# Second product of batch 1 by Strassen's algorithm as well, with a new order of the slots around it, the read-out transpose three steps later, and the last tile's column halves in two banks

## The chip, the cores and the metric

The kernel runs on one core of one Trainium2 chip. The metric is the device time in microseconds (us) of one execution; lower is better. A profile of one execution is shown beside it. Engines are named as the profile names them: PE (matmuls), PEld (its weight loads), DVE (vector), ACT (activations), POOL (GpSimd), SP (which issues DMAs). DMAs issued by POOL convert f32 to bf16 on the way.

## The reference

Attention of 8 batches between 512 tokens and 32 state rows (8 heads of 64), in both directions, and a feed-forward layer on the result:

```python
scores  = softmax(x @ state^T / 8);  xread = scores @ state     # 512 rows a batch
scores2 = softmax(state @ x^T / 8);  sread = scores2 @ x        #  32 rows a batch
rows = concat(xread, sread)          # (8*544, 512) over all heads
h = rows @ w_in                      # w_in  512 x 2048
out = gelu(h) @ w_out                # w_out 2048 x 512, exact gelu
```

## The kernel before

**One batch's path.** `rearr` (POOL, two copies) puts a loaded batch `xb` into the layout that `xtr_dma` (a DMA transpose issued by SP) turns into `xT`; `rearr_ones` puts it into a second layout `xo` for the read-out. `scores` multiplies `xT` by the state and lets ACT take exp into `e`; `norm(b, half)` (DVE: sum `cs`, reciprocal `ics`, product) makes the normalised weights `a`; `atr_dma` (SP, DMA transpose) or `atr` (PE) turns them into `AT`. Instead of forming `xread`, the kernel folds the state into `w_in` first: `p_mm` and `p_copy` make P of a batch in four chunks of 512 columns, `pmat(b, f)` or several in one `burst`; ACT copies one half of a chunk, DVE the other. The first product of hidden block m is then P^T times `AT`, two matmuls into a bank `hp` and a gelu by ACT into `g`. `M(16b+m, ...)` is that, mostly in pairs.

**The second product, plainly.** `U(u)` is a quarter (4 of 16 hidden blocks) of one of the four 128-row output tiles, four matmuls of 512 columns; after a tile's fourth quarter DVE copies the bank to `osb` and SP sends it out. Batch 0 does some of it block by block (`mm2_m`). Batches 0 and 1 are done in this way.

**The second product by Strassen.** Batches 2 to 7 split `g` and `w_out` into two by two blocks and make seven products, `X(b, name)`, 16 matmuls of 256 columns each. Their operands are sums of blocks: `g_sum` for g (DVE, one per batch and name), `w_sums` for the weights (five, once). ACT and DVE copy the products `s3`, `s34`, `q`, `oh`; POOL makes `u` and `v`; DVE adds the last ones to the bank's content. The weight sums lie in the storage of batch 0's input buffers (tags `mix0` to `mix3`).

**The read-out rows.** `sread` (PE), `sread_out` (DVE: `inv`, `srm`), then `srt`: a PE transpose into an `f` bank and a DVE copy into `XSR`. All 256 of these rows go through both products late in batch 7 (`mm1_sr`, `R`).

**Order.** Nothing is scheduled by a tool: each engine runs its instructions in the order in which the program emits them, waiting on semaphores. A batch's slot has eight steps p with one pair M each; with the pair of step p run pieces of the previous batch's second product and the next batch's preparation. In the loop over batches 2 to 7, products 4, 5, 1, 2, 7 of the batch before go with steps 0 to 4, and products 3 and 6 of the batch itself with steps 6 and 7. The slot of batch 2 before the change has two, later one, pieces U of batch 1 with steps 0 to 4, and batch 1's own slot is written out by hand with U 12 to U 22 of batches 0 and 1.

**Banks and buffers.** [...] four in turn for `hp`, `pt`, `sr`, `srT`, `p_ps` and other short uses (pool `ps_f`), four named o0 to o3 for output tiles, Strassen products and some P chunks. `xb`, `AT`, `P`, `g` have two buffers each.

**Loads.** POOL issues the loads in its own order with its copies. `hold` is a copy of one column of `g` on POOL: it makes the loads behind it wait for a certain gelu.

**The end.** For batch 7, L4, L5, L2, L1 and L7 take the place of the X products; L1 and L7 share the banks of each 128-row tile j (L7 adds on), L7 makes tile 1 in two column halves, and each half is added to `u` and sent out.

Of the kernel before, what the change touches and what calls it, by code (L numbers as in the profile page):

```python
# [17 lines left out]
def kernel(  # L18
# [84 lines left out]
    def load_w_in(f0, f1):  # L103
        for t in range(2):
            nc.gpsimd.dma_start(  # L105
                out=w_in_bf[64 * t:64 * t + 64, :, f0:f1],
                in_=moe_w_in[256 * t:256 * t + 256, f0:f1].rearrange("(c d) f -> d c f", c=HC),
            )
# [3 lines left out]
    def load_w_out(i):  # L112
        nc.gpsimd.dma_start(out=w_out_bf[:, 4 * i:4 * i + 4, :], in_=w_out_r[:, 4 * i:4 * i + 4, :])

    def load_x(b):
        xb = xin.tile([128, H, SJ * D], BF16, name="xb", tag="xb")
        nc.gpsimd.dma_start(out=xb, in_=xr[b])
        xbs[b] = xb
# [13 lines left out]

    def load_rest():
        load_w_out(1)
        for f in range(2, FC):
            load_w_in(512 * f, 512 * f + 512)
            load_w_out(f)
        load_st(2, B)
        load_x(2)
        load_x(3)  # L140


    def keep_warm(n):
# [288 lines left out]

    def burst(chunks, b_read=None):
        done = []
        first = len(chunks) < 4 and b_read is not None
        if first:
            sread(b_read)
        for i, (b, f) in enumerate(chunks):  # L440
            done.append((b, f, p_mm(b, f, ftile if i < 2 else otile)))
        for x in done[:2]:
            p_copy(*x)
        if b_read is not None and not first:
            sread(b_read)
        for x in done[2:3]:
            p_copy(*x)
        if b_read is not None:
            sread_out(b_read)
        for x in done[3:]:  # L450
            p_copy(*x)


    def pmat00(h):
        if h == 0:
            Ps[0] = att.tile([128, 2, d_ff], BF16, name="P", tag="P")
# [42 lines left out]
    def mm2(b, q, j):  # L499
        if q == 0:  # L500
            ops[b, j] = otile([128, d_model], "op")
        ps = ops[b, j]
        for m in range(4 * q, 4 * q + 4):
            nc.tensor.matmul(  # L504
                ps,
                lhsT=gs[b][:, m, j * 128:(j + 1) * 128],
                rhs=w_out_bf[:, m, :],
                start=(m == 0),
                stop=(m == MC - 1),
            )  # L510
        if q == 3:
            rows = out_rows(b, j)
            evac(ps, [(rows, slice(0, 128), 0, d_model)])

    def mm1_sr(m):
        hp = ps_f.tile([128, B * NS], FP32, name="hps", tag="f")
# [162 lines left out]
    def L2():  # L679
# [5 lines left out]
        xs[b, "v"] = c_tile("v")  # L685
        nc.vector.tensor_tensor(out=xs[b, "v"], in0=xs[b, "y"], in1=c21, op=ALU.subtract)

    def L1():
        b = B - 1
        for j in range(2):  # L690
            ps = xs[b, "x", j] = otile([128, 1, NH], "xp", 2 - 2 * j)
            x_mm(ps, xs[b, "g1"], w_sum["1"], True, (j,))
            nc.vector.tensor_tensor(
                out=xs[b, "o", 1][:, j, right],
                in0=ps[:, 0, :],
                in1=xs[b, "v"][:, j, :],
                op=ALU.add,
            )
        rows_out(1, both, right, nc.sync)

    def L7():
        b = B - 1
        o = xs[b, "o", 0]
        h = NH // 2
        for j, pieces in ((0, ((0, NH),)), (1, ((0, h), (h, NH)))):
            ps = xs[b, "x", j]
            for n0, n1 in pieces:
                for m in range(MH):
                    nc.tensor.matmul(
                        ps[:, 0, n0:n1],  # L710
                        lhsT=xs[b, "g7"][:, m, 128 * j:128 * j + 128],
                        rhs=w_sum["7"][:, m, n0:n1],
                        start=False,
                        stop=(m == MH - 1),
                        skip_group_check=True,
                    )
                nc.vector.tensor_tensor(
                    out=o[:, j, n0:n1],
                    in0=ps[:, 0, n0:n1],
                    in1=xs[b, "u"][:, j, n0:n1],  # L720
                    op=ALU.add,
                )
                eng = nc.scalar if j and n0 else nc.sync
                rows_out(0, slice(j, j + 1), slice(n0, n1), eng)

    rs = {}

# [67 lines left out]
            nc.vector.tensor_tensor(out=rs["o", 0][:, :NH], in0=ps, in1=rs["u"], op=add)  # L795
            r_out(0)

    def p_run(b, fs, banks):
        done = []
        for f, at in zip(fs, banks):  # L800
            it = iter(at or ())
            tiles = (lambda shape, name: otile(shape, name, next(it))) if at else ftile
            done.append((b, f, p_mm(b, f, tiles)))
        for x in done:
            p_copy(*x)


    def M(*ms):
# [77 lines left out]
    srt(0)  # L886
    U(4, 5)
    rearr_ones(1)
    U(6)
    pmat(0, 2)  # L890
    norm(1, 0)
# [4 lines left out]
    sread_out(1)  # L896
    M(10, 11)
    mm2_m(0, 8)
    mm2_m(0, 9)
    burst([(0, 3), (1, 0)])  # L900
    mm2_m(0, 10)
    atr(1)
    M(12, 13)
    srt(1)
    M(14, 15)
    mm2_m(0, 11)
    begin(2)
    rearr(2)
    xtr_dma(2)
    rearr_ones(2)  # L910
    U(12)
    burst([(1, 1), (1, 2)])
    U(13)
    state_prep(2, B)
    M(16, 17)
    U(14)
    M(18, 19)
    U(15)
    burst([(1, 3), (2, 0), (2, 1)])
    U(16)  # L920


    u = 17
    for p in range(2, 8):
        if p == 4:
            scores(2, 0)
            scores(2, 1)
            norm(2, 0)
            norm(2, 1)
        if p == 7:  # L930
            atr_dma(2)
        if p == 3:
            begin(3)
            rearr(3)
            xtr_dma(3)
            rearr_ones(3)
        M(16 + 2 * p, 17 + 2 * p)
        U(u)
        u += 1
        if p in (5, 7):  # L940
            pmat(2, 2 + p // 7)
        if p >= 3:
            w_sums(p - 3)
        if p == 2:
            nc.gpsimd.tensor_copy(out=hold, in_=gs[1][:, 4, 0:1])
            load_x(4)

    for b in range(2, B):
        nb = b + 1
        for p in range(8):  # L950
            k = 16 * b + 2 * p
            if p == 1 and nb < B:
                scores(nb, 0)
                scores(nb, 1)
            if p in (2, 3) and nb < B:
                norm(nb, p - 2)
            if p == 3 and nb + 1 < B:
                xtr_dma(nb + 1)
            if p == 5 and nb < B:
                atr_dma(nb)  # L960
            if p == 3 and nb < B:
                srt(b)
            if p == 7 and nb == B - 1:
                srt(nb)
            M(k, k + 1)
            if b == 2:
                for _ in range(2 if p < 4 else 1):
                    if u < 32:
                        U(u)
                        u += 1  # L970
            elif p < 5:
                if p == 0:
                    g_sum(b - 1, "5")
                X(b - 1, "45127"[p])
                if p < 3:
                    g_sum(b - 1, "127"[p])
            if nb == B and p < 4:
                for m in range(4 * p, 4 * p + 4):
                    mm1_sr(m)
            if p == 1 and nb < B:  # L980
                sread(b)
                sread_out(b)
            if p == 4 and nb == B - 1:
                sread(nb)
                sread_out(nb)
            if p == 0 and b + 3 < B:
                nc.gpsimd.tensor_copy(out=hold, in_=gs[b][:, 0, 0:1])  # L987
                load_x(b + 3)
            if p == 0 and nb + 1 < B:
                begin(nb + 1)  # L990
                rearr(nb + 1)
            if p == 2 and nb + 1 < B:
                rearr_ones(nb + 1)
            if nb == B:
                if p == 4:
                    r_homes()
                    r_sum("5")
                    r_sum("2")
                if p == 5:
                    g_sum(b, "6")  # L1000
                    R("3")
                    r_sum("1")
                    R("4")
                    r_sum("6")
                    r_sum("7")
                if p == 6:
                    R("5")
                    X(b, "3")
                    R("2")
                    R("1")  # L1010
                if p == 7:
                    R("6")
                    X(b, "6")
                continue
            if p == 5:
                g_sum(b, "6")
                if nb < B:
                    p_run(nb, (0, 1), ((0, 1), (3, 2)))
            if p == 6:
                X(b, "3")  # L1020
            if p == 7:
                if nb < B:
                    p_run(nb, (2, 3), ((1, 2), None))
                X(b, "6")
# [41 lines left out]
```

The softmax here doesn't subtract the row's maximum and nothing guards it: scores larger than these inputs give would overflow.

## Time and profile before

| | us |
|---|---|
| median of 7 runs (209.31 to 210.76) | 210.44 |
| the profiled execution: its own time | 209.73 |
| its span, first to last instruction | 208.0 |

| engine | busy, us | share |
|---|---|---|
| PE | 200.3 | 96% |
| DVE | 137.3 | 66% |
| ACT | 133.1 | 64% |
| PEld | 131.1 | 63% |
| POOL | 61.8 | 30% |

Starts and durations below come from the profiled execution. A PE row names a run of matmuls: its length ends with the last matmul's modelled end, so the step from one row's start to the next row's start is what a block takes of PE. In brackets stand the idle time ahead of a row and what ended it. A row `SPq` is the time in which SP issues a DMA, not the time until the data have landed; that is told by the view of a tile or of the DMA issues.

### The profile page before, as it was taken

What the parts mean: (1) busy time and instruction counts of PE and PEld (TensorE: products, weight loads), DVE (VectorE), ACT (ScalarE), POOL (GpSimd) and SP (SyncE); (2) the same over time, 40 slices, a digit from 0 to 9 for tenths busy, and PEclk for the clock granted to TensorE, in tenths of its full rate; (3) what the DMA queues carried; (4) which work ended last, traced back from release to release, by engine and by line L of the source; (5) the groups of instructions that cost most, each with busy time, mean ns of one, the idle gap of its engine ahead of it and who ended that gap; (6) DMA issues with size and microseconds to landing.
All of it is one profiled execution on the core that took longest, in us unless ns stands there. A gap on an engine that the chain in (4) does not pass through costs nothing.

```text
span 208.0 us, 4691 instructions
## 1 busy us (share of the span) xinstructions
PE 200.3 (96%) x1963; PEld 131.1 (63%) x1971; DVE 137.3 (66%) x218; ACT 133.1 (64%) x240; POOL 61.8 (30%) x69
## 2 busy tenths in 40 slices
PE   7799999998999999999999999999999999999993
PEld 7545444443454567756775677657775788778882
DVE  2944675747919649995699658855887553165872
ACT  3864865679794779565956777587757566744120
POOL 8964301663171015710577005500220001200000
PEclk9999999999999999999999999999999999999999
DMA  6999999789283908736681603360106001030124
GB/s 193 192 178 204 206 196 194 139 201 186 50 101 97 259 0 102 155 128 77 72 179 40 169 0 82 74 202 3 52 3 202 3 0 50 3 151 0 54 102 151
DMA packets 40261, 23.14 MB, mean 111 GB/s; under 512 B 21808, under 2 KB 38320, under 8 KB 40240
## 3 DMA queue, kind: packets, MB, share of 16 engines
q0 software_dynamic: 13936, 8.10, 28.5%
q1 hardware_dynamic: 25616, 14.36, 26.4%
q10 hardware_dynamic: 688, 0.39, 0.6%
q8 instruction: 15, 0.25, 0.5%
q14 instruction: 6, 0.05, 0.1%
HBM read 17.30 MB, written 8.91 MB: 126 GB/s over the span
## 4 chain that ended last, share of the span: by engine, by line
PE 79%; DVE 12%; POOL 4%; ACT 3%; issue 1%; POOLq 0%; DVEq 0%; ACTq 0%
PE xp L586 28%; PE hp L478 22%; PE op L504 9%; DVE gsum L580 5%; PE p_ps L415 5%; PE op L531 3%; PE hps L518 3%; PE rp L764 3%; DVE a L347 2%; POOL w_in_bf L105 2%; DVE cs L344 1%; PE sr L378 1%; PE pt L324 1%; POOL sbd L95 1%; ACT g L485 1%
## 5 line engine op out<-in xcount | busy, mean ns | idle before, releaser
L485 ACT ACTIVATE g<-hp 128x512 bf16<-128x512 f32 x124 | 67.6, 603 | 31.6 <-PE hp L478 26.5
L478 PE MATMUL hp<-AT,P 128*128 128x512 bf16 x248 | 64.2, 379 | 0.5 <-DVE XSR L405 0.4
L586 PEld LDWEIGHTS <-gsum 128*128 128x128 bf16 x464 | 45.0, 98 | 11.5 <-issue 2.1
L580 DVE TENSOR_TENSOR gsum<-g 128x2048 bf16<-128x2048 bf16 x30 | 39.3, 1327 | 0.1
L478 PEld LDWEIGHTS <-P 128*128 128x128 bf16 x248 | 22.2, 98 | 21.2 <-issue 4.0
L586 PE MATMUL xp<-ws,gsum 128*128 128x256 bf16 x272 | 32.5, 273 | 0.0
L427 DVE CAST P<-p_ps 128x512 bf16<-128x512 f32 x31 | 20.0, 683 | 16.0 <-PE p_ps L415 16.0
L504 PE MATMUL op<-w_out_bf,g 128*128 128x512 bf16 x90 | 23.0, 379 | 0.3
L586 PE MATMUL xp<-ws,g 128*128 128x256 bf16 x192 | 22.9, 273 | 0.0
L586 PE MATMUL xp<-w_out_bf,gsum 128*128 128x256 bf16 x192 | 22.8, 273 | 0.0
L586 PEld LDWEIGHTS <-g 128*128 128x128 bf16 x192 | 18.8, 98 | 4.3
L426 ACT CAST P<-p_ps 128x512 bf16<-128x512 f32 x31 | 17.0, 604 | 6.8 <-PE p_ps L415 6.8
L635 POOL TENSOR_TENSOR u<-s,oh 128x512 f32<-128x512 f32 x5 | 6.3, 1265 | 49.0 <-ACT oh L632 49.0
L504 PEld LDWEIGHTS <-g 128*128 128x128 bf16 x96 | 9.1, 98 | 11.5 <-issue 1.1
L218 POOL COPY x<-xb 128x1024 bf16<-128x1024 bf16 x12 | 12.6, 1082 | 11.1 <-DMA xb<-in_x_dram 11.1
L228 POOL COPY xo<-xb 128x1024 bf16<-128x1024 bf16 x12 | 14.5, 1242 | 1.3 <-PE sr L378 1.3
L347 DVE TENSOR_TENSOR a<-e,ics 128x512 bf16<-128x512 bf16 x14 | 13.9, 995 | 0.5
L415 PE MATMUL p_ps<-w_in_bf,sbd 64*32 64x512 bf16 x248 | 11.5, 382 | 0.8 <-ACT g L485 0.7
L344 DVE TENSOR_REDUCE cs<-e 128x16 f32<-128x512 bf16 x14 | 9.5, 676 | 3.8 <-ACT e L331 3.8
L605 POOL TENSOR_TENSOR v<-q,oh 128x512 f32<-128x512 f32 x5 | 6.4, 1275 | 14.8 <-ACT oh L637 14.8
L629 DVE TENSOR_TENSOR s<-xp,s 128x512 f32<-128x512 f32 x5 | 3.5, 692 | 11.0 <-PE xp L586 11.0
L987 POOL COPY hold<-g 128x1 bf16<-128x1 bf16 x3 | 1.0, 331 | 31.5 <-ACT g L485 31.5
(111 smaller groups left out, 220.5 us busy)
## 6 DMA issues: line engine op xcount, KB each, us to landing
xb<-in_x_dram POOLq DMA_DIRECT2D x7, 512.0 KB, 6.7
out_dram<-oh SPq DMA_DIRECT2D x13, 256.0 KB, 2.4
out_dram<-osb SPq DMA_DIRECT2D x10, 256.0 KB, 3.2
out_dram<-oh SPq DMA_DIRECT2D x5, 512.0 KB, 2.8
w_out_bf<-in_moe_w_out_dram POOLq DMA_DIRECT2D x4, 512.0 KB, 12.7
w_in_bf<-in_moe_w_in_dram POOLq DMA_DIRECT2D x6, 256.0 KB, 12.0
x0f<-in_x_dram SPq DMA_DIRECT2D x3, 256.0 KB, 4.0
w_in_bf<-in_moe_w_in_dram POOLq DMA_DIRECT2D x4, 128.0 KB, 4.2
```

The source lines that it names most:

```text
L218: nc.gpsimd.tensor_copy(out=A.x4[:, :, :, 64 * t:64 * t + 64].rearrange("p j c d -> p c j d"), in_=src[:, t],)
L228: eng.tensor_copy(out=A.xo[:, :, :, 2 + 64 * t:66 + 64 * t].rearrange("p j c d -> p c j d"), in_=src[:, t],)
L344: nc.vector.reduce_sum(out=cs, in_=e4, axis=AX.X)
L347: nc.vector.tensor_tensor(out=A.a[:, :, hs].rearrange("p g (c n) -> p g c n", n=NS), in0=e4, in1=ics[:, :, :].to_broadcast((128, G, 2, NS) ...
L415: nc.tensor.matmul(ps[t][32 * c:32 * c + 32, :], lhsT=sbd[64 * t:64 * t + 64, b, c, 32 * t:32 * t + 32], rhs=w_in_bf[64 * t:64 * t + 64, c ...
L426: nc.scalar.copy(out=dst[:, 0, :], in_=ps[0])
L427: nc.vector.tensor_copy(out=dst[:, 1, :], in_=ps[1])
L478: nc.tensor.matmul(hp, lhsT=Ps[b][:, t, m * 128:(m + 1) * 128], rhs=atts[b].AT[:, :, t, :], start=(t == 0), stop=(t == 1),)
L485: nc.scalar.activation(out=gs[b][:, m, :], in_=hp, func=AF.Gelu)
L504: nc.tensor.matmul(ps, lhsT=gs[b][:, m, j * 128:(j + 1) * 128], rhs=w_out_bf[:, m, :], start=(m == 0), stop=(m == MC - 1),)
L580: nc.vector.tensor_tensor(out=t, in0=g_q(b, h0, k0), in1=g_q(b, h1, k1), op=op)
L586: nc.tensor.matmul(ps[:, j - js[0], :], lhsT=lhs[:, m, 128 * j:128 * j + 128], rhs=rhs[:, m, :], start=(first and j == js[0] and m == 0), ...
```

## The change

- Batch 1's second product is made by the X products: 3 and 6 in its own slot, 4, 5, 1, 2, 7 in steps 0 to 4 of batch 2's slot, as for the batches after it. Its sixteen pieces U and their four evictions go.
- The slots of batches 0 (its end) and 1 are written in another order: the first pair of batch 1 comes before blocks 12 to 15 of batch 0; P's chunks, which came in bursts of two or three, come singly but for the first two of batch 1, and the last two chunks of batch 2 move into batch 2's slot; chunk 3 of batch 1 is copied by DVE alone (`p_copy_v`).
- Weight sums start earlier: sum 6 during batch 0, sums 3, 4 and 1 in batch 1, sum 7 in batch 2.
- Loads: x(2) goes ahead of the last quarter of `w_out`, the state of batch 2 is loaded alone ahead of it; x(3) and the rest of the state come after a hold on a gelu of batch 1, x(4) at step 0 of batch 2 in place of batch 1's third step, x(5) at step 6 of batch 2 in place of step 0. The rest is as it was.
- The evacuation of batch 0's last output tile goes out in two column halves.
- `srt(b)` moves from step 3 to step 6.
- In the tail, L1 and L7 take three pieces (tile 0 whole, tile 1 in two column halves) with a bank for each.

```diff
     def load_rest():
         load_w_out(1)
-        for f in range(2, FC):
-            load_w_in(512 * f, 512 * f + 512)
-            load_w_out(f)
-        load_st(2, B)
+        load_w_in(1024, 1536)
+        load_w_out(2)
+        load_w_in(1536, 2048)
+        load_st(2, 3)
         load_x(2)
-        load_x(3)
+        load_w_out(3)
...
-            evac(ps, [(rows, slice(0, 128), 0, d_model)])
+            h = d_model // 2 if j == SJ - 1 else d_model
+            evac(ps, [(rows[:, n:n + h], slice(0, 128), n, n + h) for n in range(0, d_model, h)])
...
+    PIECES = ((0, 0, NH, 2), (1, 0, NH // 2, 0), (1, NH // 2, NH, 1))
...
     def L1():
-        for j in range(2):
-            ps = xs[b, "x", j] = otile([128, 1, NH], "xp", 2 - 2 * j)
-            x_mm(ps, xs[b, "g1"], w_sum["1"], True, (j,))
+        for j, n0, n1, at in PIECES:
+            ps = xs[b, "x", j, n0] = otile([128, n1 - n0], "xp", at)
+            l_mm(ps, "1", j, n0, n1, True)
...
+    def p_copy_v(b, f, ps):
+        for t in range(2):
+            nc.vector.tensor_copy(out=Ps[b][:, t, f * 512:(f + 1) * 512], in_=ps[t])
+
+    def hold_for(b, m):
+        nc.gpsimd.tensor_copy(out=hold, in_=gs[b][:, m, 0:1])
...
     rearr_ones(1)
+    w_sums(2)
     U(6)
...
     mm2_m(0, 8)
+    p_run(1, (0, 1), (None, None))
     mm2_m(0, 9)
-    burst([(0, 3), (1, 0)])
+    atr(1)
+    pmat(0, 3)
     mm2_m(0, 10)
-    atr(1)
+    M(16, 17)
+    srt(1)
     M(12, 13)
-    srt(1)
-    M(14, 15)
     mm2_m(0, 11)
     begin(2)
     rearr(2)
     xtr_dma(2)
+    M(14, 15)
+    state_prep(2, 3)
+    pmat(1, 2)
+    hold_for(0, 15)
     rearr_ones(2)
     U(12)
-    burst([(1, 1), (1, 2)])
+    w_sums(0)
+    M(18, 19)
+    hold_for(1, 3)
+    load_x(3)
+    load_st(3, B)
     U(13)
-    state_prep(2, B)
-    M(16, 17)
+    w_sums(1)
+    M(20, 21)
+    scores(2, 0)
+    scores(2, 1)
+    w_sums(3)
     U(14)
-    M(18, 19)
+    p_run(1, (3,), ((3, 0),), p_copy_v)
+    begin(3)
+    rearr(3)
+    xtr_dma(3)
+    rearr_ones(3)
+    M(22, 23)
+    norm(2, 0)
+    M(24, 25)
+    p_run(2, (0,), ((1, 3),))
     U(15)
-    burst([(1, 3), (2, 0), (2, 1)])
-    U(16)
-    u = 17
-    for p in range(2, 8):
...
+    norm(2, 1)
+    X(1, "3")
+    atr_dma(2)
+    g_sum(1, "6")
+    M(26, 27)
+    M(28, 29)
+    p_run(2, (1,), ((1, 2),))
+    state_prep(3, B)
+    M(30, 31)
+    X(1, "6")
...
-            if p == 3 and nb < B:
+            if p == 6 and nb < B:
                 srt(b)
...
             M(k, k + 1)
-            if b == 2:
-                for _ in range(2 if p < 4 else 1):
-                    if u < 32:
-                        U(u)
-                        u += 1
-            elif p < 5:
+            if b == 2 and p in (0, 3):
+                pmat(2, 2 + p // 3)
+            if b == 2 and p == 1:
+                w_sums(4)
+            if p < 5:
...
             if p == 0 and b + 3 < B:
-                nc.gpsimd.tensor_copy(out=hold, in_=gs[b][:, 0, 0:1])
-                load_x(b + 3)
+                hold_for(b, 0)
+                load_x(4 if b == 2 else b + 3)
+            if p == 6 and b == 2:
+                hold_for(b, 12)
+                load_x(5)
```

More of the change, by code (lines that the diff above doesn't have):

```diff
@@ L430, in pmat @@
         p_copy(b, f, p_mm(b, f, ftile))
[L435 to L451, printed above, removed]
     def pmat00(h):
@@ L686, in L2, with l_mm @@
         nc.vector.tensor_tensor(out=xs[b, "v"], in0=xs[b, "y"], in1=c21, op=ALU.subtract)
+    PIECES = ((0, 0, NH, 2), (1, 0, NH // 2, 0), (1, NH // 2, NH, 1))
+    def l_mm(ps, name, j, n0, n1, first):
+        for m in range(MH):
+            nc.tensor.matmul(
+                ps,
+                lhsT=xs[B - 1, "g" + name][:, m, 128 * j:128 * j + 128],
+                rhs=w_sum[name][:, m, n0:n1],
+                start=(first and m == 0),
+                stop=(m == MH - 1),
+                skip_group_check=True,
+            )
     def L1():
         b = B - 1
-        for j in range(2):
-            ps = xs[b, "x", j] = otile([128, 1, NH], "xp", 2 - 2 * j)
-            x_mm(ps, xs[b, "g1"], w_sum["1"], True, (j,))
+        for j, n0, n1, at in PIECES:
+            ps = xs[b, "x", j, n0] = otile([128, n1 - n0], "xp", at)
+            l_mm(ps, "1", j, n0, n1, True)
             nc.vector.tensor_tensor(
-                out=xs[b, "o", 1][:, j, right],
-                in0=ps[:, 0, :],
-                in1=xs[b, "v"][:, j, :],
+                out=xs[b, "o", 1][:, j, NH + n0:NH + n1],
+                in0=ps,
+                in1=xs[b, "v"][:, j, n0:n1],
                 op=ALU.add,
@@ L702, in L7 @@
         b = B - 1
[L703 to L724, printed above, removed]
+        for j, n0, n1, at in PIECES:
+            ps = xs[b, "x", j, n0]
+            l_mm(ps, "7", j, n0, n1, False)
+            nc.vector.tensor_tensor(
+                out=xs[b, "o", 0][:, j, n0:n1], in0=ps, in1=xs[b, "u"][:, j, n0:n1], op=ALU.add
+            )
+            rows_out(0, slice(j, j + 1), slice(n0, n1), nc.scalar if n0 else nc.sync)
     rs = {}
@@ L796, in R, with p_run @@
             r_out(0)
-    def p_run(b, fs, banks):
+    def p_run(b, fs, banks, copy=None):
         done = []
@@ L804, in p_run @@
         for x in done:
-            p_copy(*x)
+            (copy or p_copy)(*x)
+    def p_copy_v(b, f, ps):
[3 more added lines that the diff above has]
+        nc.gpsimd.tensor_copy(out=hold, in_=gs[b][:, m, 0:1])
     def M(*ms):
@@ L909 @@
     xtr_dma(2)
+    M(14, 15)
+    state_prep(2, 3)
+    pmat(1, 2)
+    hold_for(0, 15)
     rearr_ones(2)
     U(12)
-    burst([(1, 1), (1, 2)])
-    U(13)
-    state_prep(2, B)
-    M(16, 17)
-    U(14)
-    M(18, 19)
-    U(15)
-    burst([(1, 3), (2, 0), (2, 1)])
-    U(16)
-    u = 17
-    for p in range(2, 8):
[L925 to L937, printed above, removed]
-        U(u)
-        u += 1
[L940 to L946, printed above, removed]
+    w_sums(0)
[3 more added lines that the diff above has]
+    load_st(3, B)
+    U(13)
+    w_sums(1)
[3 more added lines that the diff above has]
+    w_sums(3)
+    U(14)
+    p_run(1, (3,), ((3, 0),), p_copy_v)
[7 more added lines that the diff above has]
+    p_run(2, (0,), ((1, 3),))
+    U(15)
+    norm(2, 1)
[8 more added lines that the diff above has]
+    X(1, "6")
     for b in range(2, B):
@@ L965 @@
             M(k, k + 1)
-            if b == 2:
-                for _ in range(2 if p < 4 else 1):
-                    if u < 32:
-                        U(u)
-                        u += 1
-            elif p < 5:
+            if b == 2 and p in (0, 3):
[3 more added lines that the diff above has]
+            if p < 5:
                 if p == 0:
```

## The prediction

> **What bounds the kernel now.** I read the page's busy times, then its slices, then its chain, then the waits and the timelines by engine.
>
> ```profile
> PE 200.3 (96%) x1963; PEld 131.1 (63%) x1971; DVE 137.3 (66%) x218; ACT 133.1 (64%) x240; POOL 61.8 (30%) x69
> ...
> PE   7799999998999999999999999999999999999993
> ...
> PE 79%; DVE 12%; POOL 4%; ACT 3%; issue 1%; POOLq 0%; DVEq 0%; ACTq 0%
> ```
>
> PE is busy 96%; its one slice under 9 after the start is the tenth, near 50 us. So the bound is PE's own work plus few waits, and an edit is worth the matmul time it takes away plus the waits it takes away or makes. The timelines of PE (two rows), DVE and SP:
>
> ```profile
> 50.19 0.90 PE L415 MATMUL p_ps<-w_in_bf,sbd 64*32 64x512 bf16 x8 [0.67 <-ACT g L485]
> ...
> 90.40 0.59 PE L478 MATMUL hp<-AT,P 128*128 128x512 bf16 x2 [0.17 <-DVE XSR L405]
> ```
> ```profile
> 89.63 0.72 DVE L405 COPY XSR<-srT 128x128 bf16<-128x128 bf16 x1
> 89.97 0.90 DVE L608 TENSOR_TENSOR oh<-xp,v 128x512 f32<-128x512 f32 x1
> 90.78 0.68 DVE L643 TENSOR_TENSOR oh<-xp,u 128x512 f32<-128x512 f32 x1
> ```
> ```profile
> 46.89 3.18 SPq L271 DMA_TRANSPOSE xT<-x  x1
> 51.14 1.55 SPq L367 DMA_TRANSPOSE AT<-a  x1
> ```
>
> The first shows PE held while ACT switches tables for batch 2's exp. The second shows the first product waiting for the PSUM tile of srT, which DVE drains only after its normalising work; then the two adds of the Strassen product free the banks that P's matmuls want. The third shows that the transpose AT of batch 2 is issued by SP only behind xT of batch 3. It lands 3.1 to 3.4 us after issue (the view by tile), so near 54.4; the batch's first matmul starts at 55.11. **AT is nearly late already.**
>
> [...] xT holds SP 1.9 to 3.2 us and lands 4.4 to 6.4 us after issue. [...] one DVE multiply for `a` takes 0.69 us at 49 us and 1.57 at 84 us beside POOL's copies. [...] the clock is full throughout.
>
> **Prices, from starts on the PE timeline.** A pair of hidden blocks (4 matmuls, `M`) or a second-product piece (`U`) 0.864 us. A Strassen product (16 of 256 columns, `X`) 1.75. A chunk of P (8 matmuls) 0.44, and 0.22 for each further one in the same burst.
>
> **The change, part by part.**
> (1) Batch 1's second product: 16 U, 13.82 us, become 7 X, 12.25: PE -1.57. P's chunks lose bursts: before 0.66+0.66+0.87+0.44+0.44 = 3.07, after 0.66 and seven single, 3.74: +0.67. Net -0.90 of PE work. DVE gains 5 sums of 1.15 to 1.8 and four adds of 0.7 for four evictions dropped; ACT gains 3 copies of 0.59 and hands one P copy to DVE; POOL gains two adds of 1.27. DVE is 66% and ACT 64% busy; where that cover fails is in (3).
>
> (2) From 27.52 (second-product block 8 of batch 0) to batch 2's first matmul. Before: 25 blocks of 0.864 = 21.6, P 3.07, transposes, scores and state 1.29: 25.96, so 53.5 without waits; it is 55.1, so 1.6 of waits. After: 18 blocks 15.55, two X 3.50, P 2.86, the rest 1.34: 23.25. P's second chunk waits for the bank of batch 1's read-out, which DVE frees at 28.96 (+0.3), and P(1,2) for a gelu (+0.15), so PE is ready at 27.5 + 23.25 + 0.45 = 51.2. The table switch that cost 0.67 (ACT is away 3.7 us, from 45.85 to 49.54; now 40.4 to 44.1) is covered by U 14, P(1,3), two pairs, P(2,0) and U 15, 3.5 us in banks that come free in time; the X behind them needs its last gelu only at its seventh matmul.
>
> But AT is not ready. POOL now runs `hold` behind the gelu of block 15 of batch 0 (PE reaches that pair at 34.6 by the same addition; two matmuls each and ACT's queue put the gelu's end at 36.3; a hold before its load took 0.8 at 43.2), the ones-copies of batch 2 (2.0), another hold (0.3), and only then issues x(3), which before was sent off at 23.6: 39.4. Landing 5.8, as for the load issued at 43.98: 45.2. In that time POOL also issues the rest of the state (0.9), which is covered. Rearranging 2.0: 47.2. SP then: xT(3) 2.1 to 49.3, **two** half outputs of U 15 where there was one, 0.35 to 0.6 each: 50.3, and only behind them AT, +3.3: 53.6. The values it transposes are ready on DVE near 48.2 and are not what is late: what is late is SP's turn, because xT(3) stands ahead of AT and waits for POOL. So batch 2 starts at 53.7 and PE waits 2.5. Against 55.1: **-1.4**. Behind AT on SP stand only outputs of batch 1 and xT(4), needed a batch later.
>
> (3) Work moved behind that start: five X for nine U, 8.75 - 7.78 = +0.97; two P chunks +0.88; a wait of 0.1 there before goes. In that batch x(4) is loaded only at step 0 (before it was there), so POOL blocks on it: from the batch's start, load issued at +2.0, landed +7.6 (5.6 as at 57.09), then rearrange, u, ones, v begin at +7.6, 9.6, 10.9, 13.4 and v is done at +14.7. DVE's add with v, and behind it the add with u, wait for these. DVE also carries ws7 (1.2) and two P copies more, and, slowed beside POOL as at 79 to 90, ends the add with u at +16.5. P's second chunk wants that bank at +15.9: **+0.6**.
>
> (4) srt from step 3 to 6: the transpose costs the same 0.05 of PE; its bank is now drained behind P's copies, where DVE has 1 us free, and XSR is not wanted before the read-out rows at the end. Gone are the waits for it, 0.17 and 0.22, and DVE's adds come 0.36 earlier, so P's second chunk, which takes 0.9 instead of 0.56 in batches 3 and 4, loses most of its wait: -0.75 in all. No DMA moves with it.
>
> (5) The tail: L7's second half no longer waits 0.38 for DVE; L1 has 8 narrow matmuls more (+0.1), but its adds are done sooner: the last DVE add moves from 205.07 to 204.65: -0.4.
>
> (6) Other moved pieces cost nothing on the path. x(5)'s load goes to step 6 of batch 2 with a hold, about 1.5 us of POOL where POOL was idle 13.8 us (ahead of 77.04), and lands with the 6 us that the next batch's start leaves. w_sums(2) early lies in DVE's 1.5 us idle before 24.58. w_out's last part, 0.5 MB behind x(2), lands near 34.6 (x(2) 35.5 less 3.3 for 0.69 MB ahead at 205 GB/s, plus 2.6) and U 12 comes at 36. xT(2) lands by 39, scores at 39.5; if 1 us late, PE's wait for AT covers it.
>
> Sum: -1.4 + 0.97 + 0.88 - 0.1 + 0.6 - 0.75 - 0.4 = **-0.2**. The profiled execution is 209.73 (span 208.0), 0.7 under the median 210.44; the same shift on the median gives **210.2**. A measurement tells about 0.5%, 1.05 us, from no change.
>
> **Bounds of the unknown.** x(3) 5.6 to 6.7, hold 0.2 to 0.8, xT 1.9 to 3.2 on SP, outputs 0.7 to 1.2: start 53.0 to 55.4. The DVE wait in (3): 0 to 1.3. So -1.5 to +2.2. That x(3) comes at once is excluded by its place in POOL's order.
>
> **Rivals.**
> A, faster: AT is in time and the bound is PE's work. Then the start is 51.2, 2.5 earlier: 207.7. For it: PE work is 96% everywhere, and the plan has x(3) 6 us ahead of its use. Against: three sums on POOL and SP between gelu 15 and AT must shrink by 2.5 in all.
> B, slower: [...]
> C, slower: POOL's late chain in batch 2. If x(4) takes 6.7 and the ones-copies 3.5, as one pair does at 128 us, v ends at +16.8, PE waits 2.1 instead of 0.6: 211.7; it decides from a wait of 1.8. Against: both longest values at once.
>
> **How the numbers follow.** Forecast 0.58 (its own range 208.9 to 211.9; of the 0.58, 0.10 faster, 0.36 same, 0.12 slower), A 0.26, B and C 0.16. Faster 0.36, same 0.36, slower 0.28. The range cuts about a tenth at each end: 207.4 to 212.3.
>
> **What would show it.** Right: PE idle 2 to 3 us just ahead of batch 2's first pair, released by SP's AT; SP's AT row begins after two short output rows, at 50 to 51.5; x(3)'s rearranging ends near 47; no wait for XSR at 90 and 112; no wait inside the tail; the row near 50 that waits for ACT gone. Wrong: batch 2 starts by 52 (A), a PE clock under 9 near 55 (B), a PE wait over 1.5 for DVE in batch 2's sixth step (C), or PE waiting for a sum `gsum` or for ACT before 50.

## The result and the profile after

The changed kernel takes **214.84 us** (median of 12 executions, 213.15 to 216.19), the kernel before 210.37 (31 executions): ratio 1.0215, 95% interval 1.0195 to 1.0236. It is slower by 4.5 us, where 210.2 with a range of 207.4 to 212.3 was forecast. The profiled execution took 214.95, its span is 213.2.

From the page: PE, its slices, the clock granted to it, and the chain.

```profile
PE 201.7 (95%) x2022; PEld 136.7 (64%) x2027; DVE 147.5 (69%) x227; ACT 134.1 (63%) x242; POOL 70.7 (33%) x74
...
PE   8799999997499899999999999999999999999992
...
PEclk9999999999889999999999999999999999999999
...
PE 76%; DVE 9%; POOL 6%; DMA 5%; SPq 1%; issue 1%; ACT 1%; POOLq 0%; DVEq 0%
```

PE's busy time went **up** by 1.4 us although by the prediction's count there is 0.9 us less to do, so some matmuls ran longer; the clock row, 9 throughout before, has an 8 in the two slices from 53 to 64 us. Of PE's slices the tenth is 7, the eleventh 4 (53 to 59 us), and the fourteenth 8; DMA and SPq have come into the chain, and POOL has grown from 4% to 6% of it. The timelines around batch 2's start, of PE (one row of before, then after), SP and POOL:

```profile
55.11 1.04 PE L478 MATMUL hp<-AT,P 128*128 128x512 bf16 x4
```
```profile
51.51 1.92 PE L568 MATMUL xp<-ws,gsum 128*128 128x256 bf16 x16 [1.13 <-DVE gsum L562]
56.32 1.47 PE L459 MATMUL hp<-AT,P 128*128 128x512 bf16 x4 [2.89 <-DMA AT<-a]
...
58.27 2.84 PE L568 MATMUL xp<-ws,g 128*128 128x256 bf16 x16
...
74.08 0.59 PE L459 MATMUL hp<-AT,P 128*128 128x512 bf16 x2 [0.71 <-DVE P L427]
```
```profile
48.96 3.05 SPq L271 DMA_TRANSPOSE xT<-x  x1
52.10 1.01 SPq L474 DMA_DIRECT2D out_dram<-osb  x2
53.21 1.24 SPq L367 DMA_TRANSPOSE AT<-a  x1
```
```profile
39.81 0.89 POOL L117 DMA_DIRECT2D xb<-in_x_dram  x1
40.69 0.95 POOL L121 DMA_DIRECT2D st_bf<-in_state_dram  x1
46.91 2.02 POOL L218 COPY x<-xb 128x1024 bf16<-128x1024 bf16 x2 [5.27 <-DMA xb<-in_x_dram]
```

The first pair of batch 2 starts at 56.32, forecast 53.7, before 55.11, and it waits for AT as foreseen. AT's issue stands behind xT and two outputs on SP, and xT behind x(3) on POOL. The product at 58.27 takes 2.84 us where the other products of 16 matmuls take 1.9. The view of stretches says why (columns: stretch, its length, busy time and number on PE, PEld, DVE, ACT and POOL, PE's granted clock, DMA share, GB/s):

```profile
55.00:56.00 1.00, 0.00 (x0) 0.00 (x0) 0.00 (x0) 0.00 (x0) 0.00 (x0) 1.00 0.77 141
56.00:57.00 1.00, 0.68 (x3) 0.32 (x4) 0.00 (x0) 0.00 (x0) 0.00 (x0) 0.89 0.00 0
57.00:58.00 1.00, 1.00 (x10) 0.12 (x8) 0.00 (x0) 0.78 (x2) 0.19 (x1) 0.50 0.00 0
...
59.00:60.00 1.00, 1.00 (x7) 0.69 (x6) 1.00 (x2) 0.99 (x1) 0.09 (x1) 0.50 0.11 13
60.00:61.00 1.00, 1.00 (x11) 0.86 (x10) 0.26 (x1) 0.29 (x1) 0.00 (x0) 0.90 0.94 99
```

PE idles until 56.3, and from 56.8 to 60.2 its clock is 0.50. That is rival B's sign, a clock under 9 near 55.

No row of the changed kernel after 85 us has a wait of PE in brackets: the two for XSR and the one in the tail are gone. But the end is not sooner. Outputs to the time of landing (view of the DMA queues; columns: KB each, median us from issue to landing), first of after from 207.8 us, then of before from 203.2 us:

```profile
out_dram<-oh SPq DMA_DIRECT2D x1, 256.0 KB, 3.8
out_dram<-oh SPq DMA_DIRECT2D x1, 128.0 KB, 3.1
out_dram<-oh SPq DMA_DIRECT2D x1, 64.0 KB, 3.0
out_dram<-oh ACTq DMA_DIRECT2D x1, 64.0 KB, 2.5
```
```profile
out_dram<-oh SPq DMA_DIRECT2D x1, 256.0 KB, 2.5
out_dram<-oh SPq DMA_DIRECT2D x1, 128.0 KB, 1.9
out_dram<-oh SPq DMA_DIRECT2D x1, 64.0 KB, 1.7
out_dram<-oh ACTq DMA_DIRECT2D x1, 64.0 KB, 1.6
```

All four land 0.9 to 1.3 us later. I cut each span at four starts on PE: block 8 of batch 0's second product, batch 2's first pair (M32), batch 3's first pair (M48), and L1. "Last add" is from the end of the last DVE addition to the end of the span and is a part of the stage before it. The profiles of the experiments, told below, stand in the same table.

| profiled execution | to block 8 | to M32 | to M48 | to L1 | to end | last add | span |
|---|---|---|---|---|---|---|---|
| before | 27.5 | 27.6 | 20.5 | 125.2 | 7.2 | 2.6 | 208.0 |
| after | 27.7 | 28.6 | 25.2 | 124.0 | 7.7 | 3.6 | 213.2 |
| e1 (AT first) | 29.3 | 25.6 | 23.7 | 124.0 | 7.7 | 3.7 | 210.2 |
| e2 (PE kept busy) | 28.5 | 27.8 | 23.8 | 124.0 | 6.8 | 2.8 | 210.9 |
| e7 (x(3) sooner) | 28.7 | 27.0 | 23.5 | 124.0 | 8.0 | 3.9 | 211.0 |
| e5 (e1, ones 4 late) | 27.4 | 25.6 | 22.5 | 124.0 | 7.7 | 3.7 | 207.1 |
| e8 (srt and tail alone) | 28.7 | 27.6 | 20.5 | 124.1 | 6.6 | 2.6 | 207.5 |
| e9 (e5, other count) | 29.0 | 25.4 | 22.3 | 124.0 | 6.6 | 2.6 | 207.4 |

The first column wanders by 2 us between executions (27.4 to 29.3; loads at the start), in kernels that are alike there: a single profile's span says little, its later stages say much. Against before the stages of after give +0.2, +1.0, +4.7, -1.2, +0.5, in sum 5.2.

### The profile page after: what moved, and what is told of

Its sections match the earlier page's. It is cut to its first block, busy times and chain, and to the rows that moved or that the text cites. A ratio compares the mean times of both kernels' runs of the same rounds, so it can differ in the third digit from the quotient of the medians.

```text
span 213.2 us, 4826 instructions
## 1 busy us (share of the span) xinstructions
PE 201.7 (95%) x2022; PEld 136.7 (64%) x2027; DVE 147.5 (69%) x227; ACT 134.1 (63%) x242; POOL 70.7 (33%) x74
## 4 chain that ended last, share of the span: by engine, by line
PE 76%; DVE 9%; POOL 6%; DMA 5%; SPq 1%; issue 1%; ACT 1%; POOLq 0%; DVEq 0%
PE xp L568 34%; PE hp L459 20%; PE p_ps L415 4%; DMA xb<-in_x_dram 3%; PE hps L500 3%; PE op L513 3%; PE rp L744 3%; DVE a L347 2%; DVE gsum L562 2%; POOL w_in_bf L105 2%; PE op L485 2%; PE xp L674 2%; DMA AT<-a 1%; DVE cs L344 1%; PE pt L324 1%
## 5 line engine op out<-in xcount | busy, mean ns | idle before, releaser
L568 PEld LDWEIGHTS <-gsum 128*128 128x128 bf16 x528 | 51.1, 98 | 14.7 <-issue 2.3
L562 DVE TENSOR_TENSOR gsum<-g 128x2048 bf16<-128x2048 bf16 x35 | 47.8, 1383 | 0.1
L568 PE MATMUL xp<-ws,gsum 128*128 128x256 bf16 x304 | 36.4, 273 | 1.1 <-DVE gsum L562 1.1
L568 PE MATMUL xp<-ws,g 128*128 128x256 bf16 x224 | 27.7, 278 | 0.0
L568 PE MATMUL xp<-w_out_bf,gsum 128*128 128x256 bf16 x224 | 26.6, 273 | 0.0
L568 PEld LDWEIGHTS <-g 128*128 128x128 bf16 x224 | 22.3, 100 | 5.8 <-issue 0.4
L228 POOL COPY xo<-xb 128x1024 bf16<-128x1024 bf16 x12 | 18.5, 1569 | 0.0
L587 POOL TENSOR_TENSOR v<-q,oh 128x512 f32<-128x512 f32 x6 | 7.9, 1322 | 13.5 <-ACT oh L619 13.5
L415 PEld LDWEIGHTS <-sbd 64*32 64x32 bf16 x248 | 3.2, 89 | 10.3 <-issue 9.5
L590 DVE TENSOR_TENSOR oh<-xp,v 128x512 f32<-128x512 f32 x6 | 4.1, 686 | 8.0 <-POOL v L587 8.0
```

The source lines that it names most:

```text
L228: eng.tensor_copy(out=A.xo[:, :, :, 2 + 64 * t:66 + 64 * t].rearrange("p j c d -> p c j d"), in_=src[:, t],)
L415: nc.tensor.matmul(ps[t][32 * c:32 * c + 32, :], lhsT=sbd[64 * t:64 * t + 64, b, c, 32 * t:32 * t + 32], rhs=w_in_bf[64 * t:64 * t + 64, c ...
L562: nc.vector.tensor_tensor(out=t, in0=g_q(b, h0, k0), in1=g_q(b, h1, k1), op=op)
L568: nc.tensor.matmul(ps[:, j - js[0], :], lhsT=lhs[:, m, 128 * j:128 * j + 128], rhs=rhs[:, m, :], start=(first and j == js[0] and m == 0), ...
L587: nc.gpsimd.tensor_tensor(out=xs[b, "v"], in0=xs[b, "q"], in1=o[:, :, :NH], op=ALU.subtract)
```

## The experiments

Each was timed in five rounds beside the kernel before, whose median was 210.0 for e1 to e4, 210.15 for e5 to e8, 210.1 for e9 to e11 and 209.87 for e12.

**e1: AT ahead of xT(3) on SP.** In batch 1's slot:

```diff
-    xtr_dma(3)
     rearr_ones(3)
...
     atr_dma(2)
+    xtr_dma(3)
```

> The changed kernel with one line moved: SP issues AT of batch 2 ahead of xT of batch 3. Theory S (the loss is SP's order): AT leaves when the normalising is done (49.5), lands by 52.8, PE ends its product 6 at 53.3, so batch 2 starts near 53.4 in place of 56.3, and as PE is no longer idle for 3 us the clock stays at 1.0, which saves 1.6 more: 4.5 us under the changed kernel, near 210.3. Rival D (PE is held by the extra work on DVE and its banks in any case): batch 2 starts earlier, but the time comes back as waits for DVE later; at most 1.5 us gained, 213.3.

Measured 211.16 us, ratio 1.0047 [1.0022, 1.0072]: 3.7 less than after. PE, then SP:

```profile
53.08 1.92 PE L568 MATMUL xp<-ws,gsum 128*128 128x256 bf16 x16 [1.12 <-DVE gsum L562]
54.84 1.03 PE L459 MATMUL hp<-AT,P 128*128 128x512 bf16 x4
```
```profile
51.11 2.03 SPq L367 DMA_TRANSPOSE AT<-a  x1
53.23 1.88 SPq L271 DMA_TRANSPOSE xT<-x  x1
```

Batch 2 starts right behind X6, the second of batch 1's products in its own slot, without a wait for AT, and the clock stays at 1.00 there. From block 8 to M32 it is 25.6 us, 3.0 less than in after. So the cause is the place in SP's queue, not the transpose itself. What is left is PE's wait for the sum of X6, which in after lay under the wait for AT. Its time is 0.9 above the first theory's number; the waits that remain, 1.1 us for that sum and more than 1 us in step 5 of batch 2, are the matter of e5 and e6.

**e2: PE kept busy through the same wait.** Matmuls on zeros (16 ahead of X6 of batch 1, 42 behind it) into bank o1, their result unused; AT comes as late as in after.

```diff
     M(30, 31)
+    warm_in(1, 16)
     X(1, "6")
+    warm_in(1, 42)
```

> The changed kernel with matmuls on zeros that nothing uses, 16 ahead of batch 1's product 6 and 42 behind it, in a bank that is free there; they fill PE's two waits. Theory S with the clock: batch 2 still starts near 56.3, since AT lands when it did, but the granted clock stays at 1.0 from 56 to 60, and 1.6 us are saved: 213.2. Rival (the lower clock comes from something other than PE's idle time): clock still 0.5 for 3.4 us and no gain, or a little slower.

Measured 212.34, ratio 1.0113 [1.0087, 1.0139], 2.5 less than after, with the clock at 1.00 throughout the profile.

```profile
53.94 2.51 PE L798 MATMUL warm_ps<-warm 128*128 128x128 bf16 x42
56.29 1.02 PE L459 MATMUL hp<-AT,P 128*128 128x512 bf16 x4
```

M32 starts at 56.29, as in after (counted from block 8 it is 0.8 sooner, as all before it came later), and the stage behind it is 23.8 us for 25.2: the halved clock cost 1.4 us. It was also there that the tail's last landing fell from 3.6 to 2.8, which nobody had asked of 58 matmuls 150 us earlier; the two make 2.2 of the 2.5, and e9 to e11 come from the second.

**e3: before with the read-out transpose at step 6, alone.** `if p == 3 and nb < B` becomes `if p == 6 and nb < B`.

> The kernel before with srt at step 6 alone. The prediction's part 4: 0.75 us faster than before (0.36%). The trace of the changed kernel hints at 1.2 (its stretch from batch 3's start to L1 is 1.24 us shorter). Rival (DVE is as late as before, the wait only moves on): same as before within 0.2.

Measured 208.69, ratio 0.9936 [0.9914, 0.9958], -1.3 us. The span from M48 to L1 falls from 125.2 to 124.1, and both waits for XSR are gone.

**e4: before with the tail in three pieces and banks, alone.** `PIECES`, `l_mm`, `L1` and `L7` as in the change.

> The kernel before with the tail's three pieces in banks of their own alone. The prediction's part 5: 0.4 us faster. Rival (seen in the changed kernel's trace: the last add comes 0.5 us sooner after L1's start, but the last outputs land 0.9 later, since they are issued closer together): 0 to 0.5 us slower.

Measured 209.53, ratio 0.9978 [0.9961, 0.9996], -0.5 us (0.1 to 0.8 by the interval); last addition to the end 2.6. The late landing in after doesn't come from this edit.

**e5: e1 with batch 4's ones-copies behind v.**

```diff
-            if p == 2 and nb + 1 < B:
+            if p == (4 if b == 2 else 2) and nb + 1 < B:
                 rearr_ones(nb + 1)
```

> e1 with one more edit: batch 4's ones-copies on POOL (3.0 us in batch 2's slot) come behind v of batch 1 instead of ahead of it. Theory: the wait of about 1.3 us at P's chunks in step 5 of batch 2 is POOL's late chain x(4) copy, u, ones-copies, v (v ended at 70.8); with v some 3 us earlier the wait goes, 1.0 to 1.3 us less than e1's 211.2: 210.0. Rival: the DVE's own queue is the limit there [...], then v earlier gains 0.3 at most: 210.9.

Measured 209.98, ratio 0.9999 [0.9982, 1.0016], 1.2 less than e1. POOL in e1, then in e5:

```profile
66.17 3.01 POOL L228 COPY xo<-xb 128x1024 bf16<-128x1024 bf16 x2
69.14 1.70 POOL L587 TENSOR_TENSOR v<-q,oh 128x512 f32<-128x512 f32 x1
```
```profile
66.06 1.73 POOL L587 TENSOR_TENSOR v<-q,oh 128x512 f32<-128x512 f32 x1 [2.09 <-ACT oh L619]
67.73 2.02 POOL L228 COPY xo<-xb 128x1024 bf16<-128x1024 bf16 x2
```

v no longer stands behind the copies, and the stage from M32 to M48 falls by 1.2. The wait in step 5 was POOL's chain, as rival C has it, at a price between the forecast's 0.6 and C's 2.1.

**e6: e5 with batch 3's ones-copies behind gelu 14 of batch 1** (`rearr_ones(3)` with a `hold_for(1, 14)` moved ahead of X6).

> e5 with batch 3's ones-copies moved too, from beside the DVE's gsum6 to behind gelu 14 of batch 1. Theory: the 1.1 us that X6 of batch 1 waits for gsum6 come from the ones-copies that stretch norm(2,1)'s product and gsum6 (1.26 and 2.06 us, 0.7 and 1.15 alone); with them gone X6 starts some 1.0 us sooner: 209.0. Rival: gsum6 waits for the DVE queue before it in any case (norm, two casts), then 0.4 at most: 209.6.

Measured 210.03, ratio 0.9995 [0.9978, 1.0012]: nothing gained.

```profile
50.43 1.92 PE L568 MATMUL xp<-ws,gsum 128*128 128x256 bf16 x16
53.08 1.04 PE L459 MATMUL hp<-AT,P 128*128 128x512 bf16 x4 [0.73 <-DMA AT<-a]
```

The wait for the sum is gone (it took DVE 1.21 us instead of 2.06, with POOL's copies out of its way), and a wait for AT has taken its place. Neither theory had that.

**e7: after with only the load of x(3) moved ahead of batch 2's ones-copies.**

> after with only the load of x(3) moved, from behind batch 2's ones-copies and a hold to ahead of them on POOL (issued at about 36.5 instead of 39.8); SP's queue stays as in after, with xT(3) ahead of AT. Theory: AT of batch 2 is late only because xT(3), ahead of it on SP, waits for x(3); with x(3) landed by 43 to 44 xT(3) is issued by 46 to 47, AT leaves at norm(2,1)'s end (49.5) and lands by 53.5, X6's wait for gsum6 (1.1) stays the only one, the clock stays full: as e1, 211.2 (about 3.6 less than after). Rival: the load is no sooner, since the weights and inputs before it fill the DMA engines, or xT(3) waits for outputs ahead of it on SP: 213 to 215.

Measured 212.61, ratio 1.012 [1.009, 1.015], 2.2 less than after, between the two theories. The load was issued at 38.1, not 36.5, as the hold ahead of it came later, and took 7.6 us to be of use; AT left at 51.2, PE waited 1.3 for it, and the clock stayed at 1.00. A second way to shorten the same chain moves batch 2's start too, and keeps the clock.

**e8: e3 and e4 together, nothing else.**

> The kernel before with the read-out transpose at step 6 and the tail in three pieces, both and nothing else (no Strassen for batch 1). If the two gains add: 210.0 - 1.3 - 0.5 = 208.2. If they overlap (both shift the same last stage): 208.7. Against after it gives the price of the Strassen part with its reordering: 214.8 - 208.2 = 6.6 us.

Measured 208.79, ratio 0.9933 [0.9913, 0.9953], -1.4 us: e3 and e4 alone gave -1.3 and -0.5, and the intervals don't tell whether they add. Against it, the rest of the change, the Strassen part with its order, costs some 6 us.

**e9 to e11: the same edit on e5, e8 and after.** At the start 49 of 55 warming matmuls on zeros (all those in calls of three and more) become two of 64x64 each; the columns stay the same in all, and PE has 49 matmuls and 49 weight loads more.

```diff
-        for _ in range(n):
-            nc.tensor.matmul(ps[:, 0:128], lhsT=warm, rhs=warm, start=True, stop=True)
+        w = 64 if n > 2 else 128
+        for _ in range(n * 128 // w):
+            nc.tensor.matmul(ps[0:w, 0:w], lhsT=warm[:, 0:w], rhs=warm[:, 0:w], start=True, stop=True)
```

The reason is a line in the view of after's queues, stretch 208.9 to 209.4 us (packets, MB, share of 16 engines' time):

```profile
q1 hardware_dynamic: 158, 0.16, 90.7%
q8 instruction: 1, 0.02, 11.7%
```

One packet of queue q8, 16 KB of instructions, fell just where the last outputs move; 11.7% of 16 engines in 0.5 us is 0.94 us of one engine. The page has 16 such packets, 0.26 MB in all, of before 15, and before's last came at 194.1, 13.8 us ahead of its end. After has 59 matmuls and 56 weight loads more than before, and one packet more; that the count of matmuls sets the packet's place was my reading of this, which the three runs test.

> e5 with 49 of its 55 warming matmuls at the start (operands zeros, 128x128) each done as two of 64x64: 49 more matmuls, all within the first 11 us, the same columns, nothing else. Theory F: in every kernel with the Strassen product of batch 1 the last outputs land 1.1 us later because one 16 KB fetch of PE's instructions (queue q8) falls into the last 3 us (e5: 2.7 us before the end); 49 matmuls more move it some 6 us forward, out of the tail: the stretch from the last DVE addition to the end falls from 3.66 to 2.6 us, and the time by 1.0 to 209.0. Rival: the late landing comes from something else of the new order (addresses, queues), then nothing changes: 210.0, or slower by what the halved matmuls cost at the start.

> The same edit on e8 (the kernel before with the read-out transpose at step 6 and the tail), which has its last instruction fetch 11.4 us before the end. Theory F: with 49 more matmuls its count is that of e5 and after, so a 16th fetch comes about 2.8 us before the end: last addition to end from 2.57 to about 3.6, time from 208.8 to 209.8. Rival (the landing has another cause): 208.8, and the stretch stays 2.57.

> The same edit on after itself. Theory F: 214.8 to 213.8, last addition to end from 3.65 to 2.6. Rival: no change, 214.8.

The places in these texts are 1.4 us too near the end (a zero misread); the packet came 4.1 us ahead of the end in after and e5 and 12.9 in e8. The outcome:

| | time, us | ratio to before | q8 packet ahead of the end | last add to end |
|---|---|---|---|---|
| e5 | 209.98 | 0.9999 [0.9982, 1.0016] | 4.1 | 3.7 |
| e9 | 208.63 | 0.9939 [0.9913, 0.9964] | 8.7 | 2.6 |
| e8 | 208.79 | 0.9933 [0.9913, 0.9953] | 12.9 | 2.6 |
| e10 | 210.0 | 0.9993 [0.9973, 1.0014] | 4.1 | 3.9 |
| after | 214.84 | 1.0215 [1.0195, 1.0236] | 4.1 | 3.6 |
| e11 | 213.81 | 1.0153 [1.01, 1.0206] | over 5.0 | 2.9 |

The same edit makes e5 faster by 1.3 us and e8 slower by 1.2, as the packet leaves or enters the tail. After becomes faster by 1.0, but that size is not the fetch's alone: three of e11's six executions kept the full clock (211.6 to 213.2 us), of after's twelve only two (213.15 and 214.37). (e11's ratio is from the five shortest of the six.) What the fetch does there is seen in the last landing, 3.6 us and then 2.9. Eight profiles agree in their last 5.0 us: with a packet of q8 there, 4.0 to 4.1 us ahead of the end, the last landing takes 3.6 to 3.9 us (after, e5, e10), with none there 2.6 to 2.9 (before, e2, e8, e9, e11). The queues of e10 from 202.5 us to its end, and of e9 from 202.9 us:

```profile
q8 instruction: 1, 0.02, 1.1%
issues: line engine op xcount, KB each, median us to landing
out_dram<-oh SPq DMA_DIRECT2D x1, 256.0 KB, 4.1
out_dram<-oh SPq DMA_DIRECT2D x1, 128.0 KB, 3.3
```
```profile
q10 hardware_dynamic: 144, 0.07, 5.0%
issues: line engine op xcount, KB each, median us to landing
out_dram<-oh SPq DMA_DIRECT2D x1, 256.0 KB, 2.3
out_dram<-oh SPq DMA_DIRECT2D x1, 128.0 KB, 1.9
```

e10, which has none of the Strassen part, lands its outputs as late as after does; e9, which has it, lands them as early as before.

**e12: e9 with e6's move, and norm(2,1) ahead of U 15**, meant to have AT's values ready 1.3 us sooner.

> e9 with batch 3's ones-copies behind gelu 14 of batch 1 (as in e6) and norm(2,1) ahead of the P chunk and U15 on DVE. In e6 the wait of X6 for gsum6 (1.1 us) went and 0.7 us of waiting for AT took its place, since AT left only at norm(2,1)'s end (49.2). With norm(2,1) 1.3 us sooner AT leaves at about 48 and lands by 51.7, X6 ends at 52.2 and batch 2 starts there: 0.7 to 0.8 less than e9's 208.6, 207.9. Rival: the casts that come later hold PE at a bank or at P(2,0) for as long, 208.6 or more.

Measured 209.42, ratio 0.9975 [0.9956, 0.9993]: 0.8 worse than e9. PE waited 0.67 us for a bank that DVE's copy of an output tile frees and 0.86 for AT. DVE and SP show the same fault a second time:

```profile
47.59 1.52 DVE L348 TENSOR_TENSOR a<-e,ics 128x512 bf16<-128x512 bf16 x1
49.03 0.68 DVE L428 CAST P<-p_ps 128x512 bf16<-128x512 f32 x1
49.63 0.68 DVE L473 COPY osb<-op 128x512 f32<-128x512 f32 x1
```
```profile
50.33 0.81 SPq L475 DMA_DIRECT2D out_dram<-osb  x2
51.23 1.25 SPq L368 DMA_TRANSPOSE AT<-a  x1
```

AT's values are ready at 49.1, but the last two outputs of batch 0 stand ahead of AT on SP, and they wait until 50.3 for a copy that now comes behind the norm. The forecast for e12 had looked at the data and not at SP's queue.

The best measured are e9 (208.63), e3 (208.69) and e8 (208.79), 0.6 to 0.7% faster than before; they can't be told apart.

## Why the prediction was wrong, step by step

The step that failed first is (2), the start of batch 2: forecast 53.7, measured 56.3, as AT's place in SP's order was right but its chain was put 2.6 us too short. The clock fell on top of that.

| step | forecast, us | in after's profile | shown by |
|---|---|---|---|
| (2) start of batch 2 | -1.4 | +1.2 | e1, e7 |
| (3) work moved behind it | +1.85 | +1.85 | e9: +1.8 |
| halved clock | 0 (rival B) | +1.4 to +1.7 | e2: 1.4; e1 and e7: 1.5, 1.7 |
| (3) wait in step 5 less the 0.1 | +0.5 | +1.3 | the rest of its stage; e5: 1.2 |
| (4) srt | -0.75 | -1.2 | e3 |
| (5) tail, its own work | -0.4 | -0.5 | e4 |
| last landing | not thought of | +1.0 | e9 to e11 |
| sum | -0.2 | +5.1 to +5.4 | span +5.2 |

The +1.85 is the forecast's; e9, which has the moved work and no row of PE with a wait behind M32, takes 22.3 us from M32 to M48 where before takes 20.5. The sum is that of two profiles; the medians differ by 4.5.

**Step (1) was right in sign and about in size.** PE is busy for 199.5 us in e5's profile and for 200.3 in e8's: -0.8, where -0.90 was forecast. Of time less is seen: with the hazards away (e9) block 8 to M48 takes 47.7 us, with the old order (e8) 48.1, and 0.7 us of waiting for X6's sum are still in the 47.7. So the whole batch's Strassen product with its order saves about a microsecond at best; by the medians of e9 and e8 (208.63 and 208.79) nothing is shown, and this part of the change had some 6 us of ways to lose it.

**Step (2) had the right chain, link by link, and three links too short.** POOL issued x(3) at 39.8 (forecast 39.4); x(3) was of use after 7.1 us, not 5.8; xT held SP 3.05 us, not 2.1; two outputs 1.0 and AT's landing 3.1 were as forecast. In sum 2.6 us. The bounds given (5.6 to 6.7, 1.9 to 3.2) held the second and missed the first: 5.8 was a load with little beside it, while here the state's load and outputs of batch 0 moved at the same time. That these slowed it is a reading of the order of the rows; no run tested it. **The forecast had also missed that X6 waits 1.1 us for its sum**, which takes DVE 2.06 us beside POOL's copies and 1.21 without them (e6); it named that wait only under what would prove it wrong. With it PE was ready near 53.3, behind X6, and not at 51.2, so that rival A's start at 51.2 was out of reach too. In after the wait lies under the longer one, so it cost nothing; in e1 it is what is left.

**What followed from step (2) was foreseen, and priced as a mishap.** Rival B had the fall of the clock, and its sign came about; where the fall would set in and what it would cost, no run had shown before. B and C together had 0.16, and the forecast's sum had nothing for it. AT came at 56.3, forecast 53.6; the clock was at 0.50 for 3.4 us, and that cost 1.4 to 1.7.

In after the clock fell at 56.78 and rose at 60.19; of the 3.4 us ahead of the fall PE had stood idle for 2.89 and worked for 0.51. With PE kept busy there it stayed at 1.00 (e2). But the length of one wait does not decide it. Here is e11's profiled execution, whose clock stayed at 1.00:

```profile
55.21 1.04 PE L460 MATMUL hp<-AT,P 128*128 128x512 bf16 x4 [2.09 <-DMA AT<-a]
```

A wait of 1.27 us in e7 left it at 1.00 too. But in e1's profile the clock was at 0.50 from 9.6 to 13.0 us, while the loads came in, and there no wait of PE was longer than 1.5 us; PE was busy for 6.9 of the first 10 us. The trace's records of the clock change at 5.58, 56.78 and 60.19 us in after and at 4.76 and 209.56 in before, whole multiples of 3.413 us apart in each. What decides between e11's wait and after's, and where the limit lies, is not shown. Ten of after's twelve executions have a mean clock of 0.987 to 0.992 (3.4 us at half clock in 213 make 0.992), and two 1.0; those two took 213.15 and 214.37. Whether their wait was shorter is not on record.

**Step (3)'s wait was 1.4 for 0.6** (1.3 for 0.5 with the 0.1 of before), between the forecast and rival C's 2.1, because POOL's copies were slower than forecast: the ones-copies took 3.0 us in e1 and 3.5 in after instead of 2.5, and v was done 16.0 and 16.6 us behind the batch's start instead of 14.7. That DVE's work beside them slowed them was not tested by itself. **Step (4) was 0.5 too small**: the forecast counted the waits of PE that the profile names and half of the stretched P chunks, in two batches; the stage shows 1.1 to 1.2. **Step (5) was right in its sum** (-0.4, measured -0.5) and taken back by the fetch, which has nothing to do with the tail's code. Of **step (6)** nothing was seen to cost.

The places to look were well named: PE idle 2 to 3 us ahead of batch 2's first pair, released by AT, SP's AT row behind two outputs, no wait for XSR and none inside the tail, a clock under 9 near 55 as B's sign. Where AT's row stood (53.2, not 50 to 51.5) and when rearranging ended (48.9, not 47) showed the failing link.

## What to carry to other kernels

A DMA that the bottleneck engine waits for must not stand behind another that waits for something later (its place cost 3.0 us, by e1): look at the queue's order, not at when the data are ready. If a forecast has PE idle nearly as long as it was before a drop of its clock (here 2.5 us forecast, 2.89 before the drop), price the drop as likely. And before the tail of a new version is judged, see in the queue view whether an instruction fetch fell among the last outputs; 49 matmuls more at the start moved it out of the tail in e9 (last landing 2.6 us, 3.7 in e5) and e11, and into it in e10 (3.9, 2.6 in e8).

## What the runs showed that I had not expected

One 16 KB fetch of instructions, which takes 0.94 us of one of 16 DMA engines, costs 1.2 to 1.3 us of the whole kernel if it falls some 4 us ahead of the end (e10 and e9), and nothing that can be seen 8.7 us ahead of it. That it delays the outputs by standing on one of their engines is inferred from its place; that its place decides is shown by the same edit on three kernels. The time of these kernels thus stepped by 0.6% with 49 matmuls more, down (e5 to e9) or up (e8 to e10).

PE's clock was at 0.50 for 3.4 us behind a stretch of 3.4 us in which PE had stood idle for 2.89 (after), and for 3.4 us near the start of e1, where no wait of PE was longer than 1.5 us; behind a wait of 2.09 in e11 it stayed at 1.00.
